# Sliding-window attention before a mixture stage: score matmuls of six batches in 64x64 array tiles, with V copied in shifted form, and two units' x transposed on TensorE

## The chip, the cores and the metric

One core of one Trainium2 chip. The metric is the device time of one launch in microseconds (us); a time is the median of several runs with the lowest and highest in brackets. A profile is of one execution; the changed kernel's is labelled `after`. TensorE, VectorE, ScalarE and GpSimd are PE, DVE, ACT and POOL in the profile, PEld is TensorE's weight loads, SP issues DMAs.

## The reference, cut to what matters

```python
# q, k, v: (8, 8, 576, 64) float32 = batch, heads, sequence, head size
scores = (1 / sqrt(64)) * q @ k^T
rel    = pos[:, None] - pos[None, :]
mask   = (rel >= 0) & (rel < 128)                 # each query sees itself and 127 keys before it
scores = where(mask, scores - slopes[h] * abs(rel), -1e9)
attn   = softmax(scores)
x      = (attn @ v) reordered to (8 * 576, 512)
h      = x @ w_in                                 # (4608, 2048)
out    = (h * cos(h)) @ w_out                     # (4608, 512)
```

## The kernel before

Attention of one batch and the two large matmuls on a chunk of 512 tokens (the mixture stage, "MoE" in the prediction) are interleaved on TensorE. A batch has nine units: for each of four pairs of heads the first and the second 256 queries (G = 0, 1), and one tail unit for the last 64 queries of all heads. Three units are a group: its scores are one run of matmuls on TensorE, then come exp (ScalarE), a multiply with the mask (VectorE), P times V (TensorE) and the norm (VectorE).

A block of 128 queries is multiplied with two blocks of 128 keys, 256 keys for a window that needs at most 255:

```python
def scores(us):                       # whole-unit part; tr holds q and k transposed
    ...
    jobs = [(128, 384, 2 * G, 2 * G, 2), (384, 512, 2 * G + 1, 2 * G + 1, 1)]
    if G:
        jobs.append((0, 128, 2 * G - 1, 2 * G, 1))
    for (c0, c1, kc, qb, nb) in jobs:
        for x in range(2):            # two heads, on two halves of the array's rows
            ins = e.matmul(ps[:, banks[x], c0:c1], keys_ap(i, x, pr, kc),
                           query_ap(i, x, pr, qb, nb), start=True, stop=True)
    ...
def mask(b, u):                       # G == 1: one multiply of 1024 elements
    op("dve", lambda e: e.tensor_tensor(p, p, m, ALU.mult), ..., occ=605, lat=lat, pri=1)
```

The order of every engine is fixed in the program. A planner takes every operation with a planned duration (`occ`: until the next can start; `lat`: until its result is there; both in ns) and writes one fixed list for each engine. Where TensorE has nothing for an attention step yet, the planner puts w_out matmuls of an earlier chunk there. At the start, before any data is there, it lets TensorE multiply zeros (20 such matmuls):

```python
R.fill = (zop, lambda e, bank, n: e.matmul(ps[:, bank, 0:n], zero[:, 0:128], zero[:, 0:n],
                                           start=True, stop=True))
```

A unit's x, needed in transposed form by w_in, goes by a DMA transpose, or for the units in `XPE` by TensorE:

```python
XPE = [(b, u) for b in range(2) for u in range(8)]
```

The softmax here doesn't subtract the row's maximum and nothing guards it: scores larger than these inputs give would overflow.

## Time and profile before

| | kernel before |
|---|---|
| time | 313.01 us (312.55 to 313.14), 3 runs |
| span of the profiled run | 311.0 us |
| TensorE busy | 302.8 us, 97% |
| VectorE, ScalarE, GpSimd busy | 63%, 66%, 34% |

TensorE is the bound; the prediction below shows the lines for it. Lines of the windows there: length, then PE, PEld, DVE, ACT, POOL busy us with their counts, granted TensorE clock, DMA share, GB/s.

```profile
q8 instruction: 21, 0.34, 0.5%
```

### The profile page before, as it was taken

What the parts mean: (1) busy time and instruction counts of PE and PEld (TensorE: products, weight loads), DVE (VectorE), ACT (ScalarE), POOL (GpSimd) and SP (SyncE); (2) the same over time, 40 slices, a digit from 0 to 9 for tenths busy, and PEclk for the clock granted to TensorE, in tenths of its full rate; (3) what the DMA queues carried; (4) which work ended last, traced back from release to release, by engine and by line L of the source; (5) the groups of instructions that cost most, each with busy time, mean ns of one, the idle gap of its engine ahead of it and who ended that gap; (6) DMA issues with size and microseconds to landing.
All of it is one profiled execution on the core that took longest, in us unless ns stands there. A gap on an engine that the chain in (4) does not pass through costs nothing.

```text
span 311.0 us, 6735 instructions
## 1 busy us (share of the span) xinstructions
PE 302.8 (97%) x2676; PEld 177.0 (57%) x2676; DVE 196.2 (63%) x443; ACT 205.8 (66%) x300; POOL 105.7 (34%) x134
## 2 busy tenths in 40 slices
PE   7799999999989999999999999999999999999996
PEld 4478546884578558845844454455445444444444
DVE  3898666786678748874885568767874881353000
ACT  7798946886478659765885478748874984462211
POOL 8999868620007300970555046405000000000000
PEclk9999999999999999999999999999999999999999
DMA  8999999999949992999999999999823100101112
GB/s 131 170 194 192 192 171 193 157 140 173 192 70 127 153 145 70 142 146 196 113 168 174 152 169 111 150 159 138 146 64 103 36 0 34 71 0 67 70 67 101
DMA packets 160894, 39.24 MB, mean 126 GB/s; under 512 B 148960, under 2 KB 156384, under 8 KB 160864
## 3 DMA queue, kind: packets, MB, share of 16 engines
q0 software_dynamic: 109552, 18.10, 78.7%
q1 hardware_dynamic: 51312, 20.72, 36.3%
q8 instruction: 21, 0.34, 0.5%
q14 instruction: 9, 0.07, 0.1%
HBM read 36.70 MB, written 9.44 MB: 148 GB/s over the span
## 4 chain that ended last, share of the span: by engine, by line
PE 91%; DMA 4%; DVE 2%; POOL 2%; issue 0%; ACT 0%; POOLq 0%
PE ps L866 39%; PE ps L855 20%; PE ps L840 20%; PE ps L634 4%; PE ps L728 3%; DMA knat<-in_k_dram 2%; DMA xT<-xnat 2%; PE ps L731 2%; PE ps L547 1%; PE ps L714 1%; PE ps L716 1%; DVE p L689 1%; PE ps L624 1%; POOL vp L464 1%; PE ps L803 1%; DVE emtail L528 0%
## 5 line engine op out<-in xcount | busy, mean ns | idle before, releaser
L866 PE MATMUL ps<-w_outb,gT 128*128 128x512 bf16 (+2 forms) x592 | 137.9, 374 | 0.0
L832 DVE TENSOR_TENSOR gT<-ps,cos 128x512 bf16<-128x512 f32 x144 | 94.9, 686 | 28.8 <-PE ps L866 15.0
L826 ACT ACTIVATE cos<-ps,halfpi 128x512 f32<-128x512 f32 x144 | 94.9, 685 | 22.4 <-PE ps L855 7.4
L866 PEld LDWEIGHTS ps<-w_outb,gT 128*128 128x128 bf16 x592 | 52.7, 98 | 53.3 <-issue 1.6
L671 ACT ACTIVATE p<-ps 128x768 bf16<-128x768 f32 (+1 forms) x64 | 54.7, 917 | 29.7 <-PE ps L634 15.2
L855 PE MATMUL ps<-xT,w_inb 128*128 128x256 bf16 x576 | 67.6, 273 | 1.3 <-DMA xT<-xnat 1.3
L840 PE MATMUL ps<-xT,w_inb 128*128 128x512 bf16 x288 | 64.8, 379 | 0.0
L855 PEld LDWEIGHTS ps<-xT,w_inb 128*128 128x128 bf16 x576 | 54.5, 98 | 8.7 <-DMA xT<-xnat 1.6
L464 POOL DMA_DIRECT2D vp<-in_v_dram x40 | 34.7, 894 | 64.3 <-DMA xT<-xnat 36.0
L840 PEld LDWEIGHTS ps<-xT,w_inb 128*128 128x128 bf16 x288 | 27.3, 98 | 32.2 <-DVE xtail L759 1.2
L420 ACT ACTIVATE ob<-ps 128x512 f32<-128x512 f32 (+2 forms) x25 | 14.5, 582 | 43.9 <-PE ps L866 43.7
L455 POOL DMA_DIRECT2D qnat<-in_q_dram x32 | 29.2, 914 | 41.4 <-DMA xT<-xtail 40.8
L455 POOL DMA_DIRECT2D knat<-in_k_dram x32 | 29.2, 913 | 1.7 <-issue 1.7
L689 DVE TENSOR_TENSOR p<-p,emask 128x1024 bf16<-128x1024 bf16 x32 | 21.8, 685 | 11.6 <-ACT p L671 11.4
L770 DVE TENSOR_TENSOR xnat<-ps,rec 128x256 bf16<-128x256 f32 x64 | 26.7, 421 | 2.0
L728 PEld LDWEIGHTS ps<-vp,p 128*128 128x128 bf16 x256 | 17.0, 97 | 14.2 <-issue 8.8
L728 PE MATMUL ps<-vp,p 128*128 128x65 bf16 x256 | 21.9, 193 | 0.4 <-DVE p L689 0.3
L731 PE MATMUL ps<-vp,p 128*128 128x65 bf16 x192 | 20.0, 193 | 0.0
L694 DVE TENSOR_TENSOR p<-p,emask 128x256 bf16<-128x256 bf16 x32 | 9.1, 283 | 17.2 <-ACT p L671 16.7
L492 ACT ACT_TABLE_LOAD x15 | 19.2, 1283 | 0.3
L634 PE MATMUL ps<-qt,kt 64*128 64x128 bf16 (+1 forms) x320 | 18.1, 238 | 0.5 <-DVE xT L421 0.3
L634 PEld LDWEIGHTS ps<-qt,kt 64*128 64x128 bf16 x320 | 11.8, 94 | 11.7 <-issue 7.8
(58 smaller groups left out, 168.3 us busy)
## 6 DMA issues: line engine op xcount, KB each, us to landing
out_dram<-ob SPq DMA_DIRECT2D x35, 256.0 KB, 3.3
vp<-in_v_dram POOLq DMA_DIRECT2D x32, 128.0 KB, 6.1
knat<-in_k_dram POOLq DMA_DIRECT2D x25, 128.0 KB, 9.1
qnat<-in_q_dram POOLq DMA_DIRECT2D x25, 128.0 KB, 9.1
w_inb<-in_moe_w_in_dram POOLq DMA_DIRECT2D x8, 256.0 KB, 8.4
w_outb<-in_moe_w_out_dram POOLq DMA_DIRECT2D x6, 256.0 KB, 14.4
qnat<-in_q_dram POOLq DMA_DIRECT2D x3, 256.0 KB, 10.1
knat<-in_k_dram POOLq DMA_DIRECT2D x3, 256.0 KB, 13.2
```

What stands on the lines that cost most here:

```text
L455: op("pool", [lambda e: e.dma_start(nat[w][b % 2][0:rows, t, :].rearrange("p (h d) -> p h d", h=H), src[b, :, 128 * t:128 * t + rows, :].r ...
L464: op("pool", [lambda e, t=t, rows=rows: e.dma_start(vp[b % 2][0:rows, t, :, 0:64], v[b, :, 128 * t:128 * t + rows, :].rearrange("h p d -> ...
L634: ins = e.matmul(ps[:, banks[x], c0:c1], keys_ap(i, x, pr, kc), query_ap(i, x, pr, qb, nb), start=True, stop=True)
L671: op("act", lambda e: e.activation(P[i][:, :, lo:512], src_[:, :, lo:512], ACTF.Exp, scale=0.125), w=held + [("P", i)], occ=920 if u[1] el ...
L728: ins = e.matmul(o, P[i][:, x, d0:d0 + 128], V[:, kc, h, 0:65], start=True, stop=not two)
L731: ins = e.matmul(o, P[i][:, x, p0:p0 + 128], V[:, kc - 1, h, 0:65], start=False, stop=True)
L770: op("dve", lambda e: e.tensor_tensor(o, U[:, :, :, 0:64], rv[:, :, :, None].broadcast_to([128, 2, 2, 64]), ALU.mult), r=[("rec", ri)], w= ...
L826: op("act", lambda e: e.activation(cosb[ci][:, :], h, ACTF.Sin, bias=halfpi[:, 0:1]), r=["halfpi"], w=[("B", bank), ("cos", ci)], occ=586, ...
L832: op("dve", lambda e: e.tensor_tensor(o, h, cs, ALU.mult), r=[("cos", ci)], w=[("B", bank)] + keys, occ=606, lat=692, pri=3)
L840: op("pe", lambda e, kc=kc: e.matmul(ps[:, bank, :], w_in[:, kc, 128 * fc:128 * fc + 128], xT[:, kc, CH * c:CH * c + CH], start=(kc == 0), ...
L855: op("pe", lambda e, i=i, fc=fc, kc=kc: e.matmul(ps[:, bank, 256 * i:256 * i + 256], w_in[:, kc, 128 * fc:128 * fc + 128], xT[:, kc, t0:t0 ...
L866: op("pe", lambda e, fc=fc: e.matmul(ps[:, bank, 0:wd], gT[gi][:, fc, 128 * t:128 * t + 128], w_out[:, fc, c0:c0 + wd], start=(fc == 0), s ...
```

## The change

The intent: a block of 128 queries needs only 192 keys for each half of 64 queries, 128 of them common to both halves. With 64x64 tiles of the array, four matmuls run at once and skip the rest, so scores take fewer TensorE columns. P times V then needs V in two shifted forms (`vx`), which VectorE makes with eight copies a batch. Masks fall into more and smaller multiplies. x of units 2 and 3 of batch 2 moves to TensorE, to remove the one wait on a DMA in mid-kernel.

```diff
-XPE = [(b, u) for b in range(2) for u in range(8)]
+XPE = [(b, u) for b in range(2) for u in range(8)] + [(2, 2), (2, 3)]
+QUART = 2
...
+        def shifted_v(b, lo, hi, behind):
+            for j in range(2):
+                for n, t in enumerate((1 - j, j)):
+                    op("dve", lambda e, a=a, o=3 * n, t=t: e.tensor_copy(
+                        vx[a, o + lo:o + hi, :, :], V[a, t + lo:t + hi, :, :]), ...
+                       occ=70 + 180 * (hi - lo), lat=150 + 180 * (hi - lo), pri=1, behind=behind)
...
+        def quarters(b, u):              # which 64-key tile meets which queries
+            ...                          # tail: 16 pieces of 64 columns
+                for j in range(2):
+                    yield pr, j, c, Q - j, j, Q, 0, 128
+                for j in range(2):
+                    yield pr, j, c + 128, Q - 1 + j, j, Q, 64 * j, 64
...
+                    if b >= QUART:
+                        for pr, j, c, kb, ks, qb, q0, n in quarters(b, u):
+                            for x in range(2):
+                                ins = e.matmul(ps[64 * j:64 * j + 64, banks[x], c:c + n],
+                                               tr["k"][i][rows, kb, pr, 64 * ks:64 * ks + 64],
+                                               tr["q"][i][rows, qb, pr, q0:q0 + n], ...)
...                                       # mask: one multiply becomes three
+                   w=[("P", i), ("Ph", n)], occ=925 if G else 795, lat=1000 if G else 865, pri=1)
...                                       # P times V: vx in place of V, as many matmuls as before
+                            e.matmul(o, P[i][:, x, 192 * rb:192 * rb + 128],
+                                     vx[:, Q - 1, h, 0:65], start=True, stop=False)
+                            ins = e.matmul(o, Ph[hbuf[(b, u)]][:, x, rb, :],
+                                           vx[:, Q + 2, h, 0:65], start=False, stop=True)
...                                       # once: dense mask copies and zeroed Ph before batch 2
```

More of the change, by code (lines that the diff above doesn't have):

```diff
@@ L387, in bass_alibi_sliding__then__act_gcu_kernel @@
         vp = [sb(f"vp{i}", [128, NBLK, H, VW]) for i in range(2)]
-        EM = sb("emask", [128, H, 256])
+        EM = sb("emask", [128, H, 384])
         EMt = sb("emtail", [128, H, 128])
@@ L391, in bass_alibi_sliding__then__act_gcu_kernel @@
         P = [sb(f"p{i}", [128, 2, 512]) for i in range(NP)]
+        NH = 4
+        Ph = [sb(f"ph{i}", [128, 2, 2, 128]) for i in range(NH)]
+        vx = sb("vx", [128, 6, H, VW])
         Pt = [sb(f"ptail{i}", [128, 1088]) for i in range(2)]
@@ L512, in fills @@
             for i in range(2):
-                op("dve", lambda e, i=i: e.memset(vp[i][:, :, :, 64:65], 1.0), w=[("vinit", i)])
+                op("dve", lambda e, i=i: e.memset(vp[i][:, :, :, 64:66], 1.0), w=[("vinit", i)])
                 op("dve", lambda e, i=i: e.memset(vp[i][64:128, 4, :, 0:64], 0.0),
@@ L523, in masks @@
                 op("act", lambda e, h=h: e.activation(
-                    EM[:, h, :], dif[:, :, :].rearrange("p a b -> p (a b)"), ACTF.Exp,
+                    EM[:, h, 0:256], dif[:, :, :].rearrange("p a b -> p (a b)"), ACTF.Exp,
                     scale=slopes[h]), r=["dif"], w=[("EM", h)], occ=320, lat=410, table=0)
@@ L529, in tail_masks, with dense_masks @@
                     EMt[:, 4 * x:4 * x + 4, :].rearrange("p h (n f) -> p h n f", n=2),
-                    EM[:, x:H:2, :].rearrange("p h (n f) -> p h n f", n=2)[:, :, :, 0:64]),
+                    EM[:, x:H:2, 0:256].rearrange("p h (n f) -> p h n f", n=2)[:, :, :, 0:64]),
                    r=[("EM", h) for h in range(x, H, 2)], w=["EMt"], occ=330, lat=400, pri=6,
                    behind=behind)
+        def dense_masks(behind):
+            for j in range(2):
+                a, c = 64 * j, 128 - 128 * j
+                op("dve", lambda e, a=a, c=c: e.tensor_copy(
+                    EM[a:a + 64, :, 256:384], EM[a:a + 64, :, c:c + 128]),
+                   r=[("EM", h) for h in range(H)], w=[("EMd", j)], occ=330, lat=400, pri=6,
+                   behind=behind)
+            for i in range(NH):
+                op("dve", lambda e, i=i: e.memset(Ph[i][:, :, :, :], 0.0), w=[("Ph", i)],
+                   occ=200, lat=270, pri=6, behind=behind)
+        def shifted_v(b, lo, hi, behind):
+            V, i = vp[b % 2], b % 2
+            for j in range(2):
+                a = slice(64 * j, 64 * j + 64)
+                for n, t in enumerate((1 - j, j)):
+                    op("dve", lambda e, a=a, o=3 * n, t=t: e.tensor_copy(
+                        vx[a, o + lo:o + hi, :, :], V[a, t + lo:t + hi, :, :]),
+                       r=[("v", i, t + k) for k in range(lo, hi)] + [("vinit", i)],
+                       w=[("vx", n, j, k) for k in range(lo, hi)],
+                       occ=70 + 180 * (hi - lo), lat=150 + 180 * (hi - lo), pri=1, behind=behind)
         def first_transposes(w, b, g, banks):
@@ L611, in query_ap @@
             return tr["q"][i][64 * x:64 * x + 64, blk:blk + nb, pr, :]
+        def quarters(b, u):
+            if u[0] == "t":
+                for pr in range(NPAIR):
+                    for n in range(2):
+                        for j in range(2):
+                            yield pr, j, 128 * pr + 64 * n, 3 + n, j, 4, 0, 64
+                return
+            pr, G = u
+            for r in range(2):
+                Q, c = 2 * G + r, 192 * r
+                if Q == 0:
+                    for j in range(2):
+                        yield pr, j, 64, 0, j, 0, 0, 128
+                    continue
+                for j in range(2):
+                    yield pr, j, c, Q - j, j, Q, 0, 128
+                for j in range(2):
+                    yield pr, j, c + 128, Q - 1 + j, j, Q, 64 * j, 64
         def scores(us):
@@ L618, in f @@
                     banks = SLOT[s]
+                    if b >= QUART:
+                        for pr, j, c, kb, ks, qb, q0, n in quarters(b, u):
+                            for x in range(2):
+                                rows = slice(64 * x, 64 * x + 64)
+                                ins = e.matmul(ps[64 * j:64 * j + 64, banks[x], c:c + n],
+                                               tr["k"][i][rows, kb, pr, 64 * ks:64 * ks + 64],
+                                               tr["q"][i][rows, qb, pr, q0:q0 + n],
+                                               start=True, stop=True)
+                        continue
                     if u[0] == "t":
@@ L648, in scores @@
                 held += [("B", x) for x in SLOT[s]]
-                occ += 250 if u[0] == "t" else 220 if u[1] else 165
-            op("pe", f, r=keys, w=held, occ=occ, lat=occ + 165, mode=1, pri=2)
-        pcount = {"P": 0, "Pt": 0}
-        pbuf = {}
+                occ += (250 if u[0] == "t" else (165 if b >= QUART else 220) if u[1]
+                        else 140 if b >= QUART else 165)
+            op("pe", f, r=keys, w=held, occ=occ, lat=occ + 165, mode=4 if b >= QUART else 1, pri=2)
+        pcount = {"P": 0, "Pt": 0, "Ph": 0}
+        pbuf, hbuf = {}, {}
         def exps(b, u, s):
@@ L669, in exps @@
             pbuf[(b, u)] = i
+            if b >= QUART:
+                lo = 0 if u[1] else 64
+                op("act", lambda e: e.activation(P[i][:, :, lo:384], src_[:, :, lo:384],
+                                                 ACTF.Exp, scale=0.125),
+                   w=held + [("P", i)], occ=700 if u[1] else 600, lat=812 if u[1] else 710,
+                   table=phase[0], pri=1)
+                return
             lo = 0 if u[1] else 128
@@ L684, in mask, with f @@
             pr, G = u
+            if b >= QUART:
+                n = pcount["Ph"] % NH
+                pcount["Ph"] += 1
+                hbuf[(b, u)] = n
+                hh = slice(2 * pr, 2 * pr + 2)
+                p = P[i][:, :, 0:384].rearrange("p x (r f) -> p x r f", r=2)
+                def f(e):
+                    if not G:
+                        e.tensor_tensor(P[i][:, :, 64:320], P[i][:, :, 64:320],
+                                        EM[:, hh, 128:384], ALU.mult)
+                        for j in range(2):
+                            a = slice(64 * j, 64 * j + 64)
+                            ins = e.tensor_tensor(
+                                Ph[n][a, :, 1, 64 * j:64 * j + 64], P[i][a, :, 320:384],
+                                EM[a, hh, 192 * j:192 * j + 64], ALU.mult)
+                        return ins
+                    e.tensor_tensor(p[:, :, :, 0:128], p[:, :, :, 0:128],
+                                    EM[:, hh, None, 256:384].broadcast_to([128, 2, 2, 128]),
+                                    ALU.mult)
+                    for j in range(2):
+                        a = slice(64 * j, 64 * j + 64)
+                        ins = e.tensor_tensor(
+                            Ph[n][a, :, :, 64 * j:64 * j + 64], p[a, :, :, 128:192],
+                            EM[a, hh, None, 192 * j:192 * j + 64].broadcast_to([64, 2, 2, 64]),
+                            ALU.mult)
+                    return ins
+                op("dve", f, r=[("EM", 2 * pr), ("EM", 2 * pr + 1), ("EMd", 0), ("EMd", 1)],
+                   w=[("P", i), ("Ph", n)], occ=925 if G else 795, lat=1000 if G else 865, pri=1)
+                return
             p = P[i][:, :, :].rearrange("p x (r f) -> p x r f", r=2)
-            m = EM[:, 2 * pr:2 * pr + 2, None, :].broadcast_to([128, 2, 2, 256])
+            m = EM[:, 2 * pr:2 * pr + 2, None, 0:256].broadcast_to([128, 2, 2, 256])
             lat = 690 if G else 580
@@ L696, in f @@
                     return e.tensor_tensor(P[i][:, :, 256:512], P[i][:, :, 256:512],
-                                           EM[:, 2 * pr:2 * pr + 2, :], ALU.mult)
+                                           EM[:, 2 * pr:2 * pr + 2, 0:256], ALU.mult)
                 op("dve", f, r=[("P", i), ("EM", 2 * pr), ("EM", 2 * pr + 1)], w=[("P", i)],
@@ L719, in f @@
                 pr, G = u
+                if b >= QUART:
+                    for rb in range(2):
+                        for x in range(2):
+                            h, Q = 2 * pr + x, 2 * G + rb
+                            o = ps[:, ub[0], 65 * (2 * rb + x):65 * (2 * rb + x) + 65]
+                            if Q == 0:
+                                ins = e.matmul(o, P[i][:, x, 64:192], V[:, 0, h, 0:65],
+                                               start=True, stop=True)
+                                continue
+                            e.matmul(o, P[i][:, x, 192 * rb:192 * rb + 128],
+                                     vx[:, Q - 1, h, 0:65], start=True, stop=False)
+                            ins = e.matmul(o, Ph[hbuf[(b, u)]][:, x, rb, :],
+                                           vx[:, Q + 2, h, 0:65], start=False, stop=True)
+                    return ins
                 for rb in range(2):
@@ L735, in pv @@
             blocks = (3, 4) if u[0] == "t" else range(max(0, 2 * u[1] - 1), 2 * u[1] + 2)
-            op("pe", f, r=[pk, ("vinit", b % 2)] + [("v", b % 2, t) for t in blocks],
+            more = []
+            if b >= QUART and u[0] != "t":
+                blocks = () if u[1] else (0,)
+                more = [("Ph", hbuf[(b, u)])] + [("vx", n, j, k) for n in range(2) for j in range(2)
+                                                   for k in ((1, 2) if u[1] else (0,))]
+            op("pe", f, r=[pk, ("vinit", b % 2)] + [("v", b % 2, t) for t in blocks] + more,
                w=[("B", x) for x in (ub if u[0] == "t" else ub[:1])], pri=1,
@@ L812, in run @@
             scores(group)
+            if group[0][0] >= QUART and group[0][1] == (0, 0):
+                shifted_v(group[0][0], 0, 1, R.all[-1:])
             for b, u, s in group:
@@ L818, in run @@
                 i = norm(b, u, s)
+                last = R.all[-1:]
                 x_back(b, u, s, i)
+            if group[0][0] >= QUART and group[0][1] == (0, 0):
+                shifted_v(group[0][0], 1, 3, last)
         ccount = [0]
@@ L940, in bass_alibi_sliding__then__act_gcu_kernel @@
                 else:
+                    if c + 1 == QUART:
+                        dense_masks([o for o in R.all if o.eng[0] == "dve"][-1:])
                     cross_transposes(c + 1)
```

## The prediction

> **What bounds the kernel now.** I read the page's busy shares and its chain of what ended last, then the chain in order of time, the groups by shape, the windows of single stages, and the timelines of VectorE and TensorE.
>
> The page, kernel before:
>
> ```profile
> PE 302.8 (97%) x2676; PEld 177.0 (57%) x2676; DVE 196.2 (63%) x443; ACT 205.8 (66%) x300; POOL 105.7 (34%) x134
> ...
> PE 91%; DMA 4%; DVE 2%; POOL 2%; issue 0%; ACT 0%; POOLq 0%
> ```
>
> TensorE is busy 97% of the span and is 91% of the chain. A gain must come from fewer TensorE nanoseconds or from one of its few stops. 2% is 6.3 us, and TensorE is idle only 311.0 - 302.8 = 8.2 us in all, most of it at the start before any data is there.
>
> The chain in order of time, kernel before:
>
> ```profile
> 81.56 5.77 DMA xT<-xnat
> 87.38 0.50 PE ps L855 x3
> ...
> 139.67 0.75 PE ps L634 x16
> ...
> 145.51 0.58 PE ps L634 x12
> 146.09 0.23 PE ps L624 x16
> ```
>
> The first two lines are the one stop in the middle: chunk 2 of the MoE needs x of unit 3 of batch 2, whose DMA transpose took 5.77 us from issue to landing. The waits put 1.3 us on TensorE for it. The last three lines are scores of a batch: whole-unit scores (L634) and tail scores (L624), 2.1 to 2.2 us a batch with the first group.
>
> The windows, kernel before (attention of batch 4, then its MoE stage):
>
> ```profile
> 132.50:147.70 15.20, 15.20 (x152) 7.81 (x150) 9.18 (x26) 9.56 (x13) 5.13 (x7) 1.00 2.02 170
> 147.70:162.70 15.00, 15.00 (x130) 10.14 (x128) 12.85 (x25) 12.87 (x19) 8.07 (x10) 1.00 1.40 141
> ```
>
> The columns after the length are PE, PEld, DVE, ACT, POOL. TensorE is full in both stages. VectorE is busy 9.2 of 15.2 us in attention, so it has some 6 us of room there; in the MoE stage it has 2 us.
>
> The VectorE timeline in the same attention stage shows where the room lies, in front of the first mask of each of the three groups of units:
>
> ```profile
> 135.73 0.29 DVE L694 TENSOR_TENSOR p<-p,emask 128x256 bf16<-128x256 bf16 x1 [1.10 <-ACT p L671]
> ...
> 141.30 0.29 DVE L694 TENSOR_TENSOR p<-p,emask 128x256 bf16<-128x256 bf16 x1 [1.81 <-ACT p L671]
> ...
> 147.42 0.69 DVE L689 TENSOR_TENSOR p<-p,emask 128x1024 bf16<-128x1024 bf16 x1 [2.09 <-ACT p L671]
> ```
>
> Groups by shape, kernel before (busy us, mean ns of one):
>
> ```profile
> L689 DVE TENSOR_TENSOR p<-p,emask 128x1024 bf16<-128x1024 bf16 x32 | 21.8, 685 | 11.6 <-ACT p L671 11.4
> ...
> L696 DVE TENSOR_TENSOR p<-p,emask 128x512 bf16<-128x512 bf16 x32 | 13.4, 418 | 0.0
> ...
> L694 DVE TENSOR_TENSOR p<-p,emask 128x256 bf16<-128x256 bf16 x32 | 9.1, 283 | 17.2 <-ACT p L671 16.7
> ...
> L528 DVE COPY emtail<-emask 128x512 bf16<-128x512 bf16 x2 | 1.4, 718 | 0.0
> ```
>
> A mask multiply costs 0.52 ns an element plus about 150 ns, and consecutive ones overlap by about 80 ns (in the timeline a 256-wide one starts the next after 0.21 us, a 512-wide one after 0.34 us). The last line is the only bf16 copy within SBUF, and it is dear: 718 ns for 512 elements.
>
> [...] This kernel has column tiles already, the first transposes (L547, 64-wide weights). Read one by one in the trace their weight loads take 110 ns against 94 ns for L634[...], but pairs of 128-column matmuls still start 56 ns apart, the same as without column tiles (L634: 55 ns at 128 columns, 109 at 256; L624: 29 ns at 64). Two matmuls of a pair start 2 to 4 ns apart. So I take the slower weight load as hidden and four tiles as concurrent. [...] both copies ran while GpSimd issued DMAs back to back. No copy in this trace ran with GpSimd idle[...]. [...]
>
> **The change part by part.**
>
> Scores, per batch 2 to 7. Before, per pair of heads: first-half units 109 + 56 = 165 ns, second-half units 109 + 56 + 56 = 221 ns, tail 8 x 29 = 232 ns; with four of each of the two kinds 660 + 884 + 232 = 1776 ns. After, four tiles at a time: a block of 128 queries takes 56 + 29 = 85 ns, the first block of the sequence 56 ns. So 141 ns and 170 ns, and the tail has twice the matmuls on twice the tiles, 8 x 29 = 232 ns again. 564 + 680 + 232 = 1476 ns. Saved 0.30 us a batch, 1.8 us in six. The drains at the mode switches (three groups a batch, about 0.12 us each: 2.13 measured less 1.78, over three) stay. The issue rate is no limit: L547 issues a weight load and its matmul within about 4 ns. All of this is on the path.
>
> P times V: as many matmuls of 65 columns as before. Nothing.
>
> Exp on ScalarE: 768 instead of 1024 elements (810 against 1024 ns) and 640 instead of 768 (about 107 ns less by the same slope): 4 x 0.21 + 4 x 0.11 = 1.3 us less a batch, but off the path.
>
> Masks on VectorE: second-half units 0.60 us before; after, a 512-wide multiply (0.34) and two 256-wide ones on half the partitions each at full duration (0.28 each), 0.91 us. First-half units 0.55 before; after 0.34 + 2 x 0.22 (128 wide: 150 + 67), 0.78 us. Added 4 x 0.31 + 4 x 0.23 = 2.2 us a batch.
>
> Shifted copies of V: four of 528 elements and four of 1056. [...] 0.29 and 0.43 us alone, about 0.08 less where they overlap; 2 x (0.21 + 0.29) + 2 x (0.35 + 0.43) = 2.5 us a batch. VectorE in attention goes from 9.2 to about 13.9 us, against 15.2: it fits, but the room is nearly used. The first four copies (1.0 us) fall into the 1.1 to 1.8 us ahead of the first mask, the others (1.5 us) into the 1.8 us ahead of the second group. What's left, 0.7 us more masks a group, lengthens the groups; the order of instructions shows that the schedule fills this with more w_out matmuls (9, 5, 3, 6 and 4 of them in the first group of batch 2, against 8, 2, 5 and 4 in before's), of which there is a backlog (148 run in a row at the end). So no loss by itself.
>
> Extra setup in batch 2 (dense mask copies, four memsets): about 1.9 us of VectorE in a gap of 1.9 us; together with the copies it delays that first mask by perhaps 0.5 us, which one more w_out matmul and the later schedule cover.
>
> x of two units on TensorE: the stop goes away. From the last matmul's real issue (85.81 + 0.11) to 87.38 it is 1.46 us. Added: four transposes of 128 columns and their drains, about 0.25 us. Net 1.2 us gained. The x of units 0 and 1 still comes by DMA, but landed at 82.7 and 84.8, before the MoE stage began at 85.6.
>
> Sum: 313.0 - 1.8 - 1.2 = 310.0.
>
> **Rivals.** (A) Copies blocked by GpSimd. In batches 4 and 5 GpSimd issues loads until 2.4 to 3.4 us after the scores begin[...]. [...] For it: the 718 ns. Against: in batches 2, 3, 6 and 7 GpSimd is nearly idle then. It makes 1.0 us in two batches, 311.0. (B) Copies are always slow (1.4 ns an element, as L528). Then 8.7 us a batch, VectorE 20 us in a 15 us stage: it becomes the bound, TensorE waits some 4 us in each of six batches, 335 us. Against: [...] that all slow cases had GpSimd busy. 3%. (C) Four tiles don't overlap fully[...]: 144 loads of 27 ns (an estimate: 64 columns at the 0.42 ns a column of L634's matmuls), 3.9 us a batch in place of 1.5, 325 us. Against: L547's 56 ns a pair. 3%. (D) VectorE, now near full, misses the planned times slightly everywhere, 0.2 to 0.4 us of stops a batch: 311 to 312.
>
> **Range and chances.** I take half of A's loss: 310.5. Range 309.0 to 312.9: low if A costs nothing and drains shrink, high if A and D both come. Faster by over 2% would need 306.7, more than all that is removed: 2%. Slower needs B or C: 4%.
>
> **What would show it.** Right: scores with groups of about 0.5, 0.65 and 0.65 us (tail included in the last) instead of 0.60, 0.75 and 0.81; no TensorE wait on DMA of x near 85 us; copies of 528 elements near 290 ns in batches 2, 3 and 7 and longer in 4 and 5; VectorE 13 to 14.5 us in an attention stage. Wrong: TensorE waiting for VectorE (masks, copies) for over 1 us a batch; copies of 700 ns with GpSimd idle; score matmuls over 20 ns each in a row.

Some of its figures were estimates, which no line of the trace before shows: the durations of V's copies (0.29 and 0.43 us), full duration for multiplies on half the partitions, and rival A's 1.0 us. That four tiles run at once was a conclusion from pairs, and held (starts 3 to 4 ns apart). After, single copies of batches 2 and 3 took 279 to 433 ns (0.30 and 0.425 us on average over all batches); the two multiplies of 256 took 0.58 us together, against 0.28 for one on all partitions before. Its "drains at the mode switches" show in the trace before as a later start: from batch 3 on, the first w_out matmul after a group's scores starts 148 to 149 ns after the last of them, or 122 to 123 after a tail, where the paces are 56 and 29.

## More of the kernel before

```profile
145.47:164.77 19.30, 19.30 (x175) 12.38 (x174) 14.97 (x27) 16.16 (x22) 10.14 (x12) 1.00 1.48 147
```

Instructions came in 21 packets of some 16 KB, a negligible share of the DMA engines; and in this stage TensorE was busy for the whole length.

## The result, and the profile after

| | before | after |
|---|---|---|
| time, same rounds | 313.07 us (312.55 to 313.77), 4 runs | 317.91 us (315.76 to 318.25), 4 runs |
| span of the profiled run | 311.0 us | 316.2 us |
| ratio | | 1.0139, 95% interval 1.0089 to 1.0188 |

A ratio is the mean time of one kernel's fast runs over that of the other's of the same rounds, so it is not quite the ratio of the medians. The change costs 1.4%: within 2%, but 7.4 us over the predicted 310.5 and outside the range.

The page after (busy us, share, instructions; the chain that ended last; the instruction queue):

```profile
PE 301.0 (95%) x3170; PEld 177.8 (56%) x3208; DVE 222.5 (70%) x566; ACT 200.6 (63%) x305; POOL 105.7 (33%) x134
...
q8 instruction: 25, 0.41, 0.5%
...
PE 83%; DVE 6%; DMA 3%; POOL 3%; issue 3%; ACT 2%; DVEq 0%; POOLq 0%; ACTq 0%
```

TensorE does less work, as intended, and is idle for 15 us in place of 8. The chain has 3% of "issue" where it had 0: an engine waiting for nothing that the profile shows. The instruction queue brought four packets more.

The chain in order of time, scores of batch 3 after (start, us, matmuls):

```profile
107.12 0.55 PE ps L668 x36
...
112.89 0.61 PE ps L668 x44
...
119.63 0.73 PE ps L668 x64
```

The three groups' scores take 0.55, 0.61 and 0.73 us. From the first score matmul of a group to the start of the next other matmul (PE timeline), it is 0.60, 0.72 and 0.78 us before and 0.55, 0.62 and 0.73 in batch 3 of after_again, the second profile of the changed kernel, and in every batch of cal_again below, with the same scores: 2.10 and 1.90 us. So a saving is there, 0.20 us a batch.

Groups by shape, after:

```profile
L668 PE MATMUL ps<-qt,kt 64*64 64x64 bf16 x480 | 10.7, 191 | 0.0
L668 PE MATMUL ps<-qt,kt 64*64 64x128 bf16 x384 | 10.6, 222 | 0.7 <-DVE xnat L881 0.6
...
L555 DVE COPY vx<-vp 64x1056 bf16<-64x1056 bf16 x24 | 9.2, 425 | 0.1
...
L555 DVE COPY vx<-vp 64x528 bf16<-64x528 bf16 x24 | 6.3, 301 | 0.1
```

864 score matmuls in six batches, 144 a batch in place of 56. The copies of V are fast, 425 and 301 ns on average.

The windows, the same stage of batch 4 as shown of before:

```profile
151.24:174.31 23.07, 20.56 (x205) 13.36 (x208) 15.31 (x31) 15.61 (x23) 12.19 (x15) 0.93 1.55 148
```

3.8 us longer than before, at a mean granted clock of 0.93. The TensorE timeline shows why it is longer (idle time before in brackets):

```profile
155.06 0.19 PE L821 MATMUL ps<-vx,p 128*128 128x65 bf16 x1
157.55 0.20 PE L823 MATMUL ps<-vx,ph 128*128 128x65 bf16 x1 [2.29 <-issue]
...
158.80 0.24 PE L808 MATMUL ps<-vp,ptail 128*128 128x65 bf16 x1
```

In the middle of one P times V operation, between two matmuls with no semaphore between them, TensorE stops for 2.3 us. The clock is low after the stop, in the windows after it (the third column from the right is the granted clock):

```profile
157.50:158.50 1.00, 0.95 (x16) 0.71 (x17) 0.60 (x2) 0.00 (x0) 0.81 (x1) 0.98 0.51 108
158.50:159.50 1.00, 1.00 (x16) 0.80 (x13) 0.42 (x2) 0.00 (x0) 1.00 (x3) 0.50 0.19 25
159.50:161.00 1.50, 1.50 (x9) 1.04 (x8) 1.08 (x3) 0.22 (x1) 1.50 (x2) 0.50 1.63 129
161.00:164.00 3.00, 3.00 (x25) 2.51 (x24) 1.70 (x3) 2.20 (x4) 0.89 (x2) 0.85 2.18 136
```

From about 158.5 to 161.9 the clock is at half: 0.15 of the last window's 3 us is 0.45 us of loss, so 0.9 us at half speed there, 3.4 us in all, which costs 1.7 us. The matmuls of L806 and L808, 30 ns apart at first, start 50 to 60 ns apart by 158.80, and w_in matmuls of 256 columns then 213 ns apart in place of 109.

**Where the 5.2 us of span went.** I cut each trace at the first score matmul of every group. In each piece, I took the length less the time that its matmuls need at the pace of this trace (29.6 ns for 65 columns, 56, 109 and 216 ns for 128, 256 and 512). The rest is TensorE time lost.

| part | after less before, us |
|---|---|
| start, up to the first scores of batch 2 (the same TensorE work there; it took 72.1 to 74.7 us in the profiled runs; in after_thin, cal_tail and after_cal, with 73.5, 74.5 and 74.7, the granted clock was at half for 3.4 to 6.8 us between 9 and 17 us, in the others not) | +1.1 |
| third stage of batch 4: lost 4.41 against 0.32 | +4.1 |
| the other 16 pieces of batches 2 to 6 and 7's first two: lost 7.72 against 6.42 | +1.3 |
| last stage | +0.3 |
| TensorE work by these paces: scores 1.47 in place of 1.77 in each of six batches, transposes 0.22 | -1.6 |

The 6.42 holds the x stop of 1.4 us, which is gone after. So small losses grew by 7.72 - (6.42 - 1.4) = 2.7 us. Some 0.5 us of it lies in the score bursts themselves, which save 0.20 us a batch and not the 0.30 of the paces: in each group the first step takes 80 ns where the sum has 56, and the tail's steps 31 to 32 where it has 29. The other 2.2 us are waits elsewhere.

### The profile page after: what moved, and what is told of

It is laid out like the page before. It is cut to its first block, busy times and chain, and to the rows that moved or that the text cites.

```text
span 316.2 us, 7887 instructions
## 1 busy us (share of the span) xinstructions
PE 301.0 (95%) x3170; PEld 177.8 (56%) x3208; DVE 222.5 (70%) x566; ACT 200.6 (63%) x305; POOL 105.7 (33%) x134
## 4 chain that ended last, share of the span: by engine, by line
PE 83%; DVE 6%; DMA 3%; POOL 3%; issue 3%; ACT 2%; DVEq 0%; POOLq 0%; ACTq 0%
PE ps L982 34%; PE ps L971 20%; PE ps L956 18%; PE ps L668 4%; DMA w_inb<-in_moe_w_in_dram 3%; DVE xnat L881 2%; ACT p L727 2%; DVE ph L769 1%; DVE p L764 1%; POOL vp L468 1%; PE ps L821 1%; PE ps L823 1%; PE ps L573 1%; PE ps L806 1%; PE ps L688 1%
## 5 line engine op out<-in xcount | busy, mean ns | idle before, releaser
L982 PE MATMUL ps<-w_outb,gT 128*128 128x512 bf16 (+2 forms) x563 | 133.7, 373 | 3.0 <-issue 2.1
L948 DVE TENSOR_TENSOR gT<-ps,cos 128x512 bf16<-128x512 f32 x144 | 95.6, 686 | 25.5 <-ACT cos L942 16.0
L727 ACT ACTIVATE p<-ps 128x640 bf16<-128x640 f32 (+1 forms) x48 | 33.1, 757 | 26.3 <-PE ps L668 26.2
L424 ACT ACTIVATE ob<-ps 128x512 f32<-128x512 f32 (+2 forms) x28 | 16.4, 585 | 40.4 <-PE ps L982 37.5
L823 PE MATMUL ps<-vx,ph 128*128 128x65 bf16 x144 | 15.2, 193 | 2.3 <-issue 2.3
L764 DVE TENSOR_TENSOR p<-p,emask 128x512 bf16<-128x512 bf16 x24 | 10.2, 425 | 10.2 <-ACT p L727 9.7
L733 ACT ACTIVATE p<-ps 128x768 bf16<-128x768 f32 (+1 forms) x16 | 14.0, 918 | 5.3 <-PE ps L688 5.3
L555 DVE COPY vx<-vp 64x528 bf16<-64x528 bf16 (+1 forms) x48 | 15.5, 363 | 0.2
L668 PEld LDWEIGHTS ps<-qt,kt 64*64 64x64 bf16 x864 | 10.5, 108 | 8.5 <-issue 8.5
L821 PE MATMUL ps<-vx,p 128*128 128x65 bf16 x144 | 15.2, 193 | 0.0
L879 DVE RECIPROCAL rec<-ps 128x4 f32<-128x4 f32 x64 | 11.1, 175 | 5.2 <-PE ps L837 2.8
```

The costliest lines, as they stand in the source:

```text
L668: ins = e.matmul(ps[64 * j:64 * j + 64, banks[x], c:c + n], tr["k"][i][rows, kb, pr, 64 * ks:64 * ks + 64], tr["q"][i][rows, qb, pr, q0:q0 ...
L727: op("act", lambda e: e.activation(P[i][:, :, lo:384], src_[:, :, lo:384], ACTF.Exp, scale=0.125), w=held + [("P", i)], occ=700 if u[1] el ...
L821: e.matmul(o, P[i][:, x, 192 * rb:192 * rb + 128], vx[:, Q - 1, h, 0:65], start=True, stop=False)
L948: op("dve", lambda e: e.tensor_tensor(o, h, cs, ALU.mult), r=[("cos", ci)], w=[("B", bank)] + keys, occ=606, lat=692, pri=3)
L982: op("pe", lambda e, fc=fc: e.matmul(ps[:, bank, 0:wd], gT[gi][:, fc, 128 * t:128 * t + 128], w_out[:, fc, c0:c0 + wd], start=(fc == 0), s ...
```

## The experiments

Two theories. **Theory 1**: TensorE runs out of instructions. The change makes scores of many short instructions; the instruction queue brings them 16 KB at a time (records of 16384 bytes in the traces of before and after), and where a packet comes late, TensorE stops. **Theory 2**: VectorE is later than planned, through copies, masks and norms, and the fixed order makes TensorE wait. Rival A of the prediction (copies that take longer while GpSimd works) is a case of theory 2.

For theory 1 the trace has the DMA records of the instruction queue. I counted TensorE's instructions (weight loads, matmuls and waits) up to each such stop. The stops of all profiled runs, as the experiments below refer to them (before, before_look, x_only, x_again, after_cal and cal_tail have none):

```
run           instructions    stop, us             clock   fetch that ended it   restart after
              so far                               after   (DMA record, us)      the fetch's end
after          3777           155.06-157.55  2.45   0.50   154.33-156.16         1.39
after_again    3777           154.88-157.64  2.73   0.50   154.89-156.15         1.49
after_again    1985            87.13- 87.50  0.33   1.00    83.41- 86.04         1.46
cal_noshift    3777           154.34-156.79  2.34   0.50   153.39-155.32         1.47
before_split   1986            85.49- 86.71  1.20   1.00    83.67- 85.16         1.55
before_split   3777           152.79-154.33  1.44   1.00   151.67-152.62         1.71
after_shift    3777           151.35-152.05  0.67   1.00   149.40-150.56         1.49
after_shift2   4034           155.98-156.58  0.49   1.00   153.50-155.14         1.44
after_thin     4034           157.18-157.63  0.34   1.00   154.81-156.31         1.32
cal_again      4034           155.62-156.20  0.55   1.00   153.63-154.88         1.32
```

The first number is the start of the last matmul before the stop; the stop itself is the distance of the two starts less one matmul's pace. The counts 1985, 3777 and 4034 lie 7 x 256 and 256 (+1) apart, and a packet of 16384 bytes fits that with 64 bytes an instruction, an estimate from these counts (the changed kernel has 6519 TensorE instructions, 25.5 packets of 256). By it each stop is at a border between two packets, and each ends 1.3 to 1.7 us after a packet has landed; the fetches that ended them took 0.95 to 2.63 us. After the three stops of 2.34 to 2.73 us the clock was at half, after the seven of 0.33 to 1.44 us at 1.00. The instructions at the stops are quite different ones (scores, P times V, w_in).

### after_again: the changed kernel once more

> The changed kernel once more. In its trace TensorE stood still from 155.06 to 157.55 us in the middle of a unit's P times V, with no semaphore to wait for, while a 16 KB block of its own instructions was under way (DMA of the instruction queue, 154.33 to 156.15), and its clock was low just after; 4.1 us lost in that stage against 0.3 in the kernel before. Theory 1 (instructions run out): the stop is at the same place of the program in most runs, since blocks are cut at fixed places[...]: 316 to 318.5 us, sometimes less. Theory 2 (VectorE too full): the stop at 155 is an accident of one run, and the median is as before because of small waits on VectorE in every batch: 317 to 318, the stop gone from this trace without the time falling.

Measured: 317.69 us (316.24 to 318.14), ratio 1.0135 (1.0106 to 1.0164). The stop is back at the same instruction, 2.73 us long, and again with the half clock. It is no accident of one run.

### after_shift: packets moved against the work

The zero matmuls at the start are cut in four, so that 120 instructions more come before everything (60 matmuls and their loads; the texts say 115 and 114). The packet borders fall on other work. Nothing else changes.

```diff
+        def fill_parts(e, bank, n, parts=4):
+            for j in range(parts):
+                c0, c1 = n * j // parts, n * (j + 1) // parts
+                ins = e.matmul(ps[:, bank, c0:c1], zero[:, 0:128], zero[:, c0:c1], ...)
+            return ins
+        R.fill = (zop, fill_parts)
```

> The changed kernel with each warm-up matmul at the start cut into four, so that some 115 more TensorE instructions stand ahead of all the rest, at the same array time. Theory 1: the blocks of 256 instructions now end elsewhere in each batch; the fetch that came too late falls elsewhere, and the stop of batch 4 goes: 313.5 to 315 us, about 3 less than the changed kernel of the same rounds, unless another fetch becomes late. Theory 2: no effect, within 0.5 us of the changed kernel.

Measured: 315.0 us (314.42 to 316.82), ratio 1.0074 (1.004 to 1.0108), 2.7 us less than the changed kernel in the same rounds. The stop shrinks and moves into the scores (chain in order of time):

```profile
150.97 0.57 PE ps L674 x20
151.54 0.51 issue
152.05 0.41 PE ps L674 x27
```

The clock stays at 1.00 after it, and the stage loses 1.16 in place of 4.41 us. But the first group of batch 5 now loses 1.18 us in place of 0.43.

### x_only: the x part alone

```diff
-XPE = [(b, u) for b in range(2) for u in range(8)]
+XPE = [(b, u) for b in range(2) for u in range(8)] + [(2, 2), (2, 3)]
```

> The kernel before with x of units 2 and 3 of batch 2 on TensorE and nothing else. Both theories: the stop of 1.5 us before chunk 2 goes and four transposes come: 1.0 to 1.4 us less than before, 311.6 to 312.1 us. If the gain of that part was spoiled by something else in the changed kernel, this shows it; if 313 or more, the part was worth nothing.

Measured: 312.95 us (312.52 to 313.5), ratio 1.000 (0.9982 to 1.0019). In the trace the stop is gone, and the stretch from the first scores of batch 2 to the end takes 237.8 us, against 238.8 and 239.2 in two profiles of before. The times don't show this gain; see x_again.

### before_split: many short instructions, without anything else of the change

In the kernel before, score matmuls of batches 2 to 7 are cut to 64 and 32 columns: as many instructions as in the changed kernel, the same masks, no copies, full correctness. In the trace it adds 0.24 us of TensorE time a batch (0.03, 0.03 and 0.18 in the three groups without a stop).

```diff
+                    if b >= 2:
+                        for (c0, c1, kc, qb, nb) in jobs:
+                            for n in range(2 * nb):
+                                for x in range(2):
+                                    ins = e.matmul(
+                                        ps[:, banks[x], c0 + 64 * n:c0 + 64 * n + 64],
+                                        keys_ap(i, x, pr, kc), ...)      # 64 columns
```

> The kernel before with the score matmuls of batches 2 to 7 cut into 64 columns (tail 32), still 64x128 tiles: as many TensorE instructions as the changed kernel (144 weight loads and matmuls a batch in place of 56), the same masks, no copies of V, all order as before. Theory 1: instructions alone can make a late fetch: up to 2 to 4 us slower than before if one of the blocks ends badly, and in any case fewer instructions left at the start of some fetch; at least 0.6 us from the short matmuls. Theory 2: VectorE is as before, so at most 0.6 to 1 us slower.

Measured: 316.31 us (314.12 to 317.02), ratio 1.0095 (1.0055 to 1.0134). Chain in order of time, both places:

```profile
85.66 1.04 issue
...
153.06 1.27 issue
```

Two stops of 1.20 and 1.44 us, at packet borders, with VectorE's work as before and small waits as before (1.94 and 1.85 us in the six first and six second groups, against 1.96 and 1.86). So the instructions alone make the stops. The first cost nothing here: the wait on x, 1.4 us in the same piece before, is gone, and the piece is 20.34 us long in both. The second cost some 1.4 us (its piece is 1.63 longer, 0.18 of it short matmuls), and the short matmuls 1.4 us in six batches. This is what theory 1 says and theory 2 can't give. After these two shorter stops the clock stays at 1.00.

### before_look: a second profile of the kernel before

> The kernel before once more, for its trace. Taking x of two units onto TensorE gave no time though its trace showed 1.0 us less from batch 2 on. Either the first 72 us, which hold no change, differ from run to run (72.1 in the first trace of before, 73.5 in x_only): then this trace has them anywhere between 72 and 73.6; or the 1.46 us stop on the DMA of x in the first trace was a long one: then it is 0.2 to 1 us here. The time as before, 312.5 to 313.8.

Measured: 313.56 us. The stop on x is there again, 1.77 us; the start took 72.6 us.

### after_shift2: packets moved further

The zero matmuls are cut in six, 200 instructions ahead in place of 120 (190 and 114 in the text).

> As after_shift, but some 190 more TensorE instructions ahead in place of 114. Theory 1: in four traces TensorE ran dry exactly after 3777 of its instructions (448 + 13 x 256 + 1), in the burst of scores and P times V of batch 4; with 190 more ahead that point lies before the third scores of batch 4, where some 20 instructions a us run, so no dry stop there: 0.5 to 1 us less than after_shift, 313.8 to 314.6. What then remains over the kernel before is Theory 2, VectorE's waits. Theory 2 alone: as after_shift.

Measured: 314.63 us (314.53 to 315.2), ratio 1.0044 (1.0016 to 1.0073). The large stop is gone; one of 0.49 us is left, one packet further. What is left of the loss is mostly theory 2, as the next runs show. The VectorE timeline at batch 5's first group:

```profile
170.57 1.65 DVE L562 COPY vx<-vp 64x528 bf16<-64x528 bf16 x4
```

The same stretch in the windows (PE, PEld, DVE, ACT, POOL):

```profile
170.60:172.30 1.70, 1.54 (x14) 0.77 (x9) 1.67 (x6) 1.67 (x4) 1.70 (x3) 1.00 2.14 180
```

And TensorE's timeline after it:

```profile
173.16 0.22 PE L825 MATMUL ps<-vp,p 128*128 128x65 bf16 x2 [0.47 <-DVE ph L767]
```

The four copies take 1.65 us, with GpSimd busy for the whole of 1.70 us. In batch 3 of the changed kernel, where GpSimd was busy 0.15 of 1.10 us, they take 1.00 us. The masks come late, and TensorE waits with the first P times V until they are done.

### after_thin: the copies made tiny

after_shift2 with V's copies of batches 3 to 7 of two elements. Its output is wrong, which doesn't matter for the time. Relative error 0.87; number and order of instructions stay.

```diff
-                        vx[a, o + lo:o + hi, :, :], V[a, t + lo:t + hi, :, :]),
+                        vx[a, o + lo:o + hi, 0:H if b == QUART else 1, 0:VW if b == QUART else 2],
+                        V[a, t + lo:t + hi, 0:H if b == QUART else 1, 0:VW if b == QUART else 2]),
```

> As after_shift2, same order of every engine, but the shifted copies of V of batches 3 to 7 copy only two elements a block (wrong result on purpose). If the copies are what makes TensorE wait in batches 3 to 7: the waits of the second and third groups (0.2 to 0.4 us each) and the 0.9 us of batch 5 shrink, 1 to 1.8 us less than after_shift2. If the longer chain of mask, P times V and norm makes it wait, the waits stay and the gain is under 0.5 us.

Measured: 315.43 us (313.56 to 316.13), ratio 1.0055 (1.0013 to 1.0097), not told apart from after_shift2; its start took 73.5 us in the profile against 72.2, with 3.4 us of half clock in it. From batch 2 on it took 239.3 against 240.4 us. VectorE in the same place:

```profile
171.62 0.71 DVE L562 COPY vx<-vp 64x2 bf16<-64x2 bf16 x4
```

The loss of batch 5's first group falls from 1.07 to 0.27 us, so the copies beside GpSimd cost 0.8 us there. But the second groups still lose 0.41 to 0.56 us each, the third groups of batches 3, 5 and 6 0.48 to 0.61: that is not the copies.

### after_cal: planned durations nearer to the measured ones

after_shift2 with planned durations nearer to the measured ones. The masks of a unit had started 0.95 and 0.82 us before the next instruction (VectorE timeline) where 0.925 and 0.795 were planned. Four copies of 528 elements were planned at 1.00 us, which they took with GpSimd idle, against 1.28 to 1.80 beside it: now 1.24. The norm gets 50 ns of slack. The dense masks of batch 2 move into the stage before.

```diff
-                       occ=70 + 180 * (hi - lo), lat=150 + 180 * (hi - lo), ...
+                       occ=200 + 110 * (hi - lo), lat=280 + 110 * (hi - lo), ...
-                   ..., occ=925 if G else 795, lat=1000 if G else 865, pri=1)
+                   ..., occ=960 if G else 825, lat=1035 if G else 895, pri=1)
-               occ=340, lat=425, pri=0)                               # the norm
+               occ=340 if b < QUART else 390, lat=425 if b < QUART else 475, pri=0)
```

> As after_shift2, but the planned durations of VectorE's masks, copies and norms set to what the traces show (a mask 30 to 35 ns longer than planned, a norm about 50), and the dense masks and memsets of batch 2 made during the MoE stage before it. If the remaining loss is misplaced work (TensorE's fixed order puts too few w_out matmuls ahead of a wait on VectorE), it goes: 1.5 to 2 us less than after_shift2, 312 to 313, at or a little below the kernel before. If VectorE is really too full, no better than after_shift2. The new order may also make another block of instructions come late: then a dry stop is in its trace.

Measured: 312.63 us (311.42 to 313.17), ratio 0.997 (0.9938 to 1.0001), 2.0 us less than after_shift2 in the same rounds. First and second groups lose about 0.25 us each (the first of batch 4 0.52), where second groups had lost 0.41 to 0.56 and the first of batch 2 1.05. So 30 to 60 ns more for masks, norms and the first copies, and one move, took most of the small waits away. The third groups still lose about 0.47 us, against 0.24 to 0.36 before; no run took that apart, nor which of these edits did how much.

### cal_again: the same file, five rounds

> The recalibrated change of before, the same file, once more with five rounds, to settle whether it beats the kernel before. Both causes taken away (instruction supply moved on by the cut warm-up, small waits by planned times that fit), what is left of the change should show: 1.8 us of scores and 1.2 us of the x stop, less some 1 us of added transposes, drains and 0.1 us a group that no plan took away. Expected 311.5 to 312.8, ratio 0.995 to 0.999; first scores of batch 2 to end of span 236 to 237.5 us against 238.8 to 239.2 of before. If the earlier 312.63 was luck of the start, the ratio is over 1.000.

Measured: 311.11 us (310.86 to 312.66), ratio 0.9944 (0.9926 to 0.9962) against 313.18 of before. This beats the kernel before by 0.6%. The page's chain and the stage of batch 4 in the windows:

```profile
PE 94%; DMA 2%; POOL 2%; issue 0%; DVE 0%; ACT 0%; POOLq 0%
```

```profile
150.54:170.62 20.08, 19.68 (x210) 12.60 (x209) 15.89 (x32) 15.83 (x22) 9.28 (x11) 1.00 1.71 148
```

The 16 pieces of the table above lose 5.01 us in place of 7.72. The copies still take 1.31 and 1.69 us in batches 4 and 5, but there TensorE no longer waits for them.

### cal_noshift: the new plan, with the packets where they were

cal_again with the zero matmuls whole, as in the changed kernel.

> The recalibrated plan without the cut warm-up: the instruction blocks of TensorE now lie as in the changed kernel. If instruction supply is the large part (theory 1), TensorE runs dry again at the same count of its instructions (3777) in batch 4 and loses 1 to 4 us there: 314 to 316.5 us. If planned times and waits on VectorE were the large part (theory 2), it stays within 0.5 us of the run with the cut warm-up, 312 to 313.

Measured: 313.72 us (311.36 to 314.98), ratio 1.0011 (0.9979 to 1.0043), in the same rounds as cal_again. Chain and windows of the same stage:

```profile
154.61 2.18 issue
```

```profile
150.86:174.21 23.35, 21.17 (x210) 13.50 (x209) 15.99 (x33) 15.82 (x22) 12.59 (x15) 0.93 1.77 150
```

The stop is back at instruction 3777, now within a w_in matmul's stream, and so is the low clock. The stage loses 4.27 us against 1.00 in cal_again; from batch 2 on, every other piece loses the same within 0.03 us. Across runs the time comes and goes: three runs took 314.5 to 315.0 us with mean clocks of 0.989 to 0.995, the other three 311.4 to 312.9 with 0.999 and more. In the changed kernel, of eight runs, the five with 0.994 or 0.995 took 317.5 to 318.3 us, and of three at 1.000 two took 315.8 and 316.2. That fits a stop of varying length, but the mean clock alone does not show one: after_cal, after_thin and cal_tail were profiled at 0.989 and 0.995 with the half clock only in the first 17 us.

### cal_tail: fewer instructions

cal_again with the tail scores in their form of before, the same TensorE time. The text on record says 64 instructions fewer a batch; it is 32 (16 matmuls and their loads).

```diff
-                    if b >= QUART:
+                    if b >= QUART and u[0] != "t":
```

> The recalibrated plan with the cut warm-up, and the tail scores of batches 2 to 7 back in their form of before (64 keys more to a tile): the same 232 ns of TensorE work, but 64 instructions fewer a batch. If instruction supply still costs something (theory 1), fewer instructions give up to 0.5 us less: 311.5 to 312.5. But all later blocks shift against the data DMA as well, so a new dry stop of up to 1 us is possible. If supply is of no more weight, equal to the recalibrated one within 0.3 us, plus at most 0.1 us a batch for one more switch of tile shape inside the third group.

Measured: 311.98 us (310.81 to 313.59), ratio 0.9967 (0.9944 to 0.9989). No stop for instructions is left in its profile: batch 4's third stage loses 0.52 us in place of 1.00. The third stages of batches 3, 5 and 6 lose 0.06 us more, with one more switch of tile shape in each, for which up to 0.1 was expected. The times don't tell it from cal_again; its profiled start took 74.5 us, 2 us longer, with the clock at half from 12.2 to 15.6 us.

### x_again: the x part alone, five rounds

> Only the x part of the change (two units of batch 2 on TensorE), with five rounds to see a gain under 0.3%. By the prediction's step 1.2 us less than before, ratio 0.996, near 311.8. By the earlier three rounds 1.000 within 0.002. If the ratio is again 1.000, what the stop gave is taken back elsewhere or lost in the spread of the start.

Measured: 312.97 us (312.06 to 313.19), ratio 0.9988 (0.9976 to 1.0). The page's chain:

```profile
PE 94%; DMA 2%; POOL 2%; DVE 1%; issue 0%; ACT 0%; POOLq 0%
```

DMA is 2% of it in place of 4%. From batch 2 on the trace takes 237.80 us, the same as x_only, 1.0 to 1.4 us less than before. The times show 0.4 us less, with none not excluded. In both profiled runs of it the start was later (73.0 and 73.5 us against 72.1 and 72.6 of before), although the instructions are the same up to there and the clock was full. Whether that is chance stays open.

## Why the prediction was wrong

- **Scores: right in kind, a third short.** Predicted 0.30 us a batch less, a sum of paces; measured 0.20 (2.10 to 1.90 us), so 1.2 us in six batches in place of 1.8. Four tiles do run at once (starts 3 to 4 ns apart), so rival C is out.
- **The stop on x: right in the trace** (1.4 us gone, transposes 0.22 us); in the times at most 0.8 us of it is seen.
- **Masks and copies: close.** Masks of a second-half unit took 0.95 us (predicted 0.91), the two multiplies on half the partitions 0.58 of it, each at full duration as charged, of a first-half unit 0.82 (0.78). Four copies of 528 elements took 1.00 us in batches 2 and 3 as predicted, four of 1056 1.55 (1.5). Rival B is out.
- **The step that failed: "The issue rate is no limit: L547 issues a weight load and its matmul within about 4 ns."** It asked whether TensorE can issue that fast, not whether instructions arrive that fast. The change puts 88 more load and matmul pairs into each batch, 1056 more instructions, four packets. The third group alone uses 128 instructions in 0.73 us, half a packet. At the border to the packet in question in batch 4:

```
kernel   256 instructions left at   fetch            left at its start, at its end
before          142.16 us           147.50-148.47         120, 90
after           147.83 us           154.33-156.16          17, none
```

  From 256 left to the fetch it was about as long in both (5.3 and 6.5 us). The kernel before used 136 instructions in that time, the changed one 239. It stopped for 2.45 us, and then ran for 3.4 us at half the clock: together 4.1 us more than before. The prediction's sum has no term for it; the three ways to undo it (after_shift, after_shift2, cal_again against cal_noshift) each gave 2 to 3 us back in the times (after_shift2 by its ratio, 1.0044 against 1.0135), and before_split made it without the rest of the change.
- **"So no loss by itself" also failed, by a size.** This is rival D, which was given 0.2 to 0.4 us a batch and not put into the sum: measured 2.7 us in six batches, 0.5 of it the scores' shortfall above and 2.2, near 0.4 each, waits. The largest single part (1.04 against 0.33 us in the first group) is in batch 2, where the dense masks and memsets stood in the way, which "one more w_out matmul" was to cover. Planned times nearer to the measured ones and the dense masks made earlier brought the 16 pieces to 5.01 us, what before loses without the stop on x.
- **Rival A: the copies did take longer beside GpSimd, where they met.** Four copies of 528 elements took 1.28 to 2.12 us in batch 4 and 1.00 to 1.76 us in batch 5, and, not foreseen, up to 1.70 us in batch 6, the longer ones all while GpSimd was busy; with GpSimd idle 1.00 to 1.02. They cost 0.8 us in one batch of after_shift2. In the changed kernel's own profiled run the stop for instructions had moved batch 5 behind GpSimd's work, and there they took 1.00 us.
- **Range and chances.** They didn't follow from the terms: A and D in full give 313.4, over the stated 312.9, and "slower needs B or C" has 4% where B and C have 3% each. Neither changes the outcome.

With both causes taken away, the time is 311.11 us, 0.6 from the 310.5 predicted. That is in part luck: the scores' term was 0.6 us too large, and the new plan made up for it, with 0.25 us lost in a first or second group where the kernel before loses 0.25 to 0.42. What isn't settled is why the packet is late. Data DMAs were under way at that time (transposes of x took 6.2 us from issue to landing there), but no run took them away.

## What to carry to other kernels

When a change replaces long instructions by many short ones, count instructions as well as nanoseconds: how many an engine uses in the densest microsecond (here 128 in 0.73 us), against how many are left when the next packet lands (here none). A stop with "issue" as its only reason, in the middle of an operation and always at the same instruction count, is a sign of it; shift the count by some harmless instructions ahead and see whether it moves. In a kernel with a fixed order, put measured durations into the plan before judging a change, since some 30 ns too little a step went with waits of 0.2 to 0.6 us a group here.
